# A two-branch transformer block on one core: early loads on one queue, eleven normalisations on GpSimd, a second value/key split, and a new order of work

## The chip, the cores and the metric

The kernel runs on one core of a Trainium2 chip. The core has a matrix engine (TensorE, "PE" in the profile, with its weight loads "PEld"), VectorE ("DVE"), ScalarE ("ACT"), GpSimd ("POOL"), SyncE ("SP", used here to issue DMAs), and 16 DMA engines. The metric is the device time of one execution in microseconds (us), lower is better. A difference of about 1% (2 us) is what a measurement of this kernel can tell from no change.

## What is computed

`x` is 2048 rows of 448 values (16 tiles of 128 rows, numbered 0 to 15 below). The block is a linear attention with softmax features, and then a gated MLP:

```
h  = x + attention(layernorm(x))
h2 = h + mlp(layernorm(h))

attention: q, k, v = split of x @ wqkv into 16 heads of 28
           phi(t)  = [softmax(t @ w_phi), softmax(-(t @ w_phi))]
           kv = sum over rows of phi(k)^T v ;  z = sum over rows of phi(k)
           o  = (phi(q) @ kv) / (phi(q) . z + 1e-6) ;  return o @ wo
mlp:       (sigmoid(x @ w_gate) * (x @ w_up)) @ w_down        inner width 1792
```

## The kernel before

The program is a graph of 887 named tasks. A task is written in this document by its name and numbers, as in `xn 7`. `_Graph.task` notes a task's engine (or, with `engs`, the engines that it may run on), what it depends on, and which PSUM banks it may take. `_Graph.stored` (line 132) reads the table `ORDER` (line 40): each number is 32 times the task's index, plus 4 times the number of the bank choice, plus the number of the engine choice. Dealt out by engine, the table gives the queue of each engine; an engine works its queue strictly in that order. `emit` (line 253) puts a semaphore wait before a task for each thing that it depends on. `TURNS` (line 90) adds pairs: the first task of a pair waits for the second as well, and nothing else depends on it. Within TensorE's queue waits are left out, except where the second half of a product follows its first half ("after", line 278).

The work goes through these stages.

The lead. Loads of `x` (`load_x`, in groups of two or four tiles), of the key, value and query columns of `wqkv` (`wk`, `wv`, `wq`), and of `w_phi` (`wph`) are issued on SP; three of them (`x 0`, `wk 1`, `x 6`) on ACT. The key and query weights are multiplied with `w_phi` once: TensorE transposes the key columns (`kT`, line 545), ACT copies them (`WkT`), TensorE multiplies (`wM`, line 560; `wM 1 b` for the keys, `wM 0 b` for the queries) with a masked `w_phi` (`Wp 0`, `Wp 1`, line 529), and ACT or VectorE copies the product out (`W2`). For a tile of `x`: statistics `bst`, `agg` on VectorE (588, 590), `ve` and `rstd` (591, 593: variance plus epsilon, to the power of -1/2, on GpSimd), the normalisation `xn` (line 608 on VectorE, 607 on ACT, which needs the negated mean `mm`, `nm` of lines 596 and 598), and the transpose into `xnT`: tiles 0 to 3 on TensorE (`xP`, 618) with a copy `xT`, the others in pairs by a DMA transpose on SP (`xT`, 626). TensorE's clock starts low, so dummy matmuls of a zero tile are put into its queue: `warm` (537) and 15 `fill` (993).

The key/value stage. `pair_of` (line 636) makes two products of 14 matmuls in all that run side by side on the two halves of the array, the first 8 as the task `pa` (or `va`) and the last 6 as `pb` (`vb`). A tile's key and value are one such pair; for the tiles in `VV` (line 584: tiles 0 and 1) the values of both tiles are one pair (`va 0`, `vb 0`) and the keys of both another (`pa 0`, `pb 0`). A pair takes two banks, which come free when what is in them has been read. Per tile follow `ekp`, `ekm` (exponentials, ACT), `v1` (a copy of the values), `ss` (sums, VectorE, 683), `rs` (687), `phi` (689, VectorE or GpSimd) and `kv` (16 matmuls into bank 4, line 701). Query products `qa`, `q` (741) for four tiles at a time and their exponentials `eqp`, `eqm` (751) run in between.

The bridge. After `kv 15`: `kvz` (756, VectorE), `num` (777: 16 matmuls for a tile), its copy `ocp` (line 784, ACT or VectorE), and for each pair of tiles `rSm`, `rr`, `b`, `c`, `rd`, `o` (lines 793 to 805, VectorE), the transpose of `o` (pair 0 on TensorE, `oP`, and `oT`; the others by DMA, `od` and `oT` on SP, 826), the product with `wo` (`woa`, `wo_`, 838), the residual and its statistics, `ve2`, `rstd2`, `hn`, and a second transpose (`hP`/`hT`, or `hT` on SP).

The MLP. `ga`, `gu` (939: gate and up, 70 pairs), `sig` (ACT), `hh` (956, VectorE), `dn` (973: 14 matmuls for a tile), `fin` (980, VectorE), `st` (the store, SP). The columns of the last tile's `dn 15` are cut in two (line 966), so that the first half is finished and stored while the second is computed.

Dealt out, the queues before begin as follows.

```
SP    x2 wk0 wph x4 wq2 wq3 wq1 wq0 x8 wv1 wv0 wom6 wqT1 wqT0 x12 wom4 xT4 ...
ACT   x0 wk1 x6 WkT3 WkT0 WkT1 WkT2 W2_1_3 W2_1_0 W2_1_2 W2_1_1 xT0 xT3 xT2 ekp0 ...
DVE   warm0 dmask bst3 bst2 agg3 agg2 ve2 bst1 bst0 Wp1 agg0 xn3 xn2 agg1 bst6 bst7 bst5
      xn0 xn1 agg6 bst4 xT1 agg5 agg4 agg7 ve4 mm4 bst8 ...
POOL  ... maskW rstd2 Wp0 ve0 ve1 rstd0 rstd1 rstd4 nm4 mm8 ve8 rstd8 kvz1 nm8 phi0 phi1 mm12
      rstd12 nm12 phi3 phi5 phi7 phi8 phi9 phi10 phi11
PE    warm0, 11 fills, kT3 kT0 kT1 kT2 wM13 wM10 wM11 xP3 wM12 fill xP0 xP1 kv0 xP2 3 fills
      pa0 pb0 pa3 va0 pb3 vb0 pa2 wM01 pb2 wM00 wM02 wM03 pa5 pa4 pb5 pb4 pa6 kv0 kv1 pb6 ...
```

Of the kernel before, what the change touches and what calls it, by code (L numbers as in the profile page):

```python
# [86 lines left out]
"""  # L87


TURNS = [(('phi', 0), ('xn', 8)), (('rstd', 12), ('xn', 11)), (('phi', 7), ('phi', 6)), (('phi', 11), ('phi',  # L90
         12)), (('rstd2', 2), ('hn', 2))]


class _Task:
    __slots__ = ("name", "eng", "occ", "lat", "fn", "deps", "rank", "kind", "banks", "until", "got",
                 "start", "finish", "idx", "bias", "need", "size", "after", "rows", "pace", "behind", "engs")


class _Graph:
# [934 lines left out]
```

## Time and profile before

| | |
|---|---|
| median of 3 runs | 205.72 us (205.47, 205.72, 206.79) |
| span of the profiled execution | 202.7 us (the profile gives no other time for it) |
| TensorE busy | 196.8 us, 97% of the span, 2279 matmuls |
| VectorE, ScalarE, GpSimd busy | 134.2, 93.3 and 31.2 us |
| chain of work that ended last | 91% TensorE, 4% VectorE, 2% DMA |
| first key/value product starts | 11.78 us |
| first gate product starts | 63.93 us |

The span is the time from the first to the last instruction of the profiled execution. The run's time is 3.0 us longer (205.72 less 202.7), for what lies around the span; the profiled execution is taken to be like the median one. Times in rows are us from the span's start. In a row of the timeline the two first columns are start and duration, then engine, line, operation, output and inputs, and how many instructions were merged; in brackets the idle time before, and what ended it.

### The profile page before, as it was taken

The numbers are of one execution on the slowest core, as the hardware profiler recorded it, in microseconds if no ns is written. First come the engines' busy times: TensorE is split into PE (matmuls) and PEld (weight loads), VectorE is DVE, ScalarE is ACT, GpSimd is POOL, SyncE is SP. The second block draws the span as 40 slices with busy tenths as digits, with TensorE's granted clock in tenths as the row PEclk, the third lists the DMA queues.
The fourth block names the chain that finished last, engine by engine and source line by source line (L and its number), as shares of the span: only waits on it lengthen the run. The fifth ranks groups of instructions, "written<-read, shape, count | busy, mean of one in ns | idle before, by whom it ended". The sixth has DMA issues, their size and how long they took to land.

```text
span 202.7 us, 5397 instructions
## 1 busy us (share of the span) xinstructions
PE 196.8 (97%) x2279; PEld 110.0 (54%) x2279; DVE 134.2 (66%) x305; ACT 93.3 (46%) x168; POOL 31.2 (15%) x51
## 2 busy tenths in 40 slices
PE   7899999998999999999999999999999999999994
PEld 2545554555347985555444444454444455895553
DVE  3999999987999985697968754443335305542132
ACT  2669998899999553343212432201352300442000
POOL 5526747720000110002000110000001000000000
PEclk9999999999999999999999999999999999999999
DMA  6998968733050097100262000040000500000222
GB/s 185 307 279 132 261 168 205 248 102 97 0 133 19 3 158 192 45 0 3 52 155 55 0 3 0 0 105 3 0 0 3 144 0 5 0 3 0 93 91 91
DMA packets 35109, 16.94 MB, mean 84 GB/s; under 512 B 26828, under 2 KB 34060, under 8 KB 35084
## 3 DMA queue, kind: packets, MB, share of 16 engines
q1 hardware_dynamic: 34460, 16.07, 32.5%
q10 hardware_dynamic: 624, 0.52, 0.8%
q8 instruction: 18, 0.29, 0.6%
q14 instruction: 7, 0.06, 0.1%
HBM read 8.98 MB, written 1.84 MB: 53 GB/s over the span
## 4 chain that ended last, share of the span: by engine, by line
PE 91%; DVE 4%; DMA 2%; issue 1%; SPq 0%
PE bank L939 42%; PE bank L973 21%; PE bank L642 11%; PE bank L838 5%; PE bank L741 5%; DMA wphd<-in_A_w_phi_dram 2%; PE bank L701 2%; PE bank L777 1%; DVE opm L430 1%; DVE st L588 1%; DVE xn_pad L608 1%; PE bank L560 0%; PE bank L618 0%; DVE rSm L793 0%; SPq L466 0%
## 5 line engine op out<-in xcount | busy, mean ns | idle before, releaser
L939 PE MATMUL bank<-xnT,wg_sb 64*128 64x512 bf16 (+1 forms) x490 | 87.6, 333 | 0.2 <-issue 0.2
L939 PE MATMUL bank<-xnT,wu_sb 64*128 64x512 bf16 (+1 forms) x490 | 87.6, 333 | 0.0
L948 ACT ACTIVATE sg_sb<-bank 128x512 f32<-128x512 f32 (+1 forms) x70 | 34.3, 514 | 80.8 <-PE bank L939 70.2
L956 DVE SCALAR_TENSOR_TENSOR hh<-sg_sb,bank 128x512 bf16<-128x512 f32 (+1 forms) x70 | 38.9, 575 | 29.2 <-ACT sg_sb L948 29.0
L939 PEld LDWEIGHTS bank<-xnT,wg_sb 64*128 64x128 bf16 x490 | 45.1, 94 | 18.9 <-issue 1.5
L939 PEld LDWEIGHTS bank<-xnT,wu_sb 64*128 64x128 bf16 x490 | 45.0, 94 | 15.4
L973 PE MATMUL bank<-wd_sb,hh 128*128 128x448 bf16 (+1 forms) x238 | 43.1, 342 | 0.0
L973 PEld LDWEIGHTS bank<-wd_sb,hh 128*128 128x128 bf16 x238 | 22.9, 98 | 20.1 <-issue 1.1
L980 DVE SCALAR_TENSOR_TENSOR x_sb<-bank,x_sb 128x448 bf16<-128x448 f32 (+1 forms) x17 | 9.9, 595 | 26.4 <-PE bank L973 26.4
L642 PE MATMUL bank<-Wk,xnT 64*128 64x448 bf16 x112 | 22.4, 350 | 0.1
L642 PE MATMUL bank<-Wv,xnT 64*128 64x448 bf16 x112 | 21.9, 350 | 0.0
L683 DVE TENSOR_REDUCE ssum<-ek 128x32 f32<-128x896 bf16 x16 | 16.6, 1060 | 0.5 <-ACT ek L662 0.4
L751 ACT ACTIVATE eq<-bank 128x1024 bf16<-128x1024 f32 x16 | 16.5, 1053 | 0.1
L689 POOL TENSOR_TENSOR phi<-ek,rsum 128x896 bf16<-128x896 bf16 x9 | 15.1, 1691 | 6.8 <-PE bank L701 2.9
L741 PE MATMUL bank<-xnT,Wq 64*128 64x512 bf16 x112 | 14.6, 377 | 0.6 <-ACT opm L430 0.5
L430 ACT CAST opm<-bank 128x960 bf16<-128x960 f32 x14 | 13.1, 979 | 1.0 <-PE bank L777 1.0
L878 POOL TENSOR_TENSOR rs<-rs,neghalf 128x2 f32<-128x2 f32 x8 | 5.5, 697 | 51.5 <-DVE rs L876 46.7
L838 PE MATMUL bank<-wo_sb,oT 64*128 64x448 bf16 x112 | 13.2, 350 | 0.0
L642 PEld LDWEIGHTS bank<-Wk,xnT 64*128 64x128 bf16 x112 | 9.1, 94 | 6.3 <-issue 0.6
L642 PEld LDWEIGHTS bank<-Wv,xnT 64*128 64x128 bf16 x112 | 9.2, 94 | 4.3
L588 DVE BATCH_NORM_STATS2 st<-x_sb 128x6 f32<-128x448 bf16 x16 | 9.1, 607 | 2.0 <-DMA x_sb<-in_A_x_dram 2.0
L664 ACT ACTIVATE ek<-bank 128x448 bf16<-128x448 f32 x16 | 9.2, 585 | 1.6 <-PE bank L642 1.6
(92 smaller groups left out, 168.6 us busy)
## 6 DMA issues: line engine op xcount, KB each, us to landing
...
wd_sb<-in_B_w_down_dram SPq DMA_DIRECT2D x7, 224.0 KB, 2.9
...
x_sb<-in_A_x_dram SPq DMA_DIRECT2D x2, 224.0 KB, 3.9
x_sb<-in_A_x_dram ACTq DMA_DIRECT2D x2, 224.0 KB, 4.0
```

The lines of the kernel that those rows point to most:

```text
L430: return e.copy(dst, src) if hasattr(e, "activation") else e.tensor_copy(dst, src)
L588: task(("bst", t), "dve", dve(D), lambda e, t=t: e.bn_stats(st1[:, t % 4, :], X(t)), [x_ld[t], opt(("agg", t - 4))])
L642: r = e.matmul(bank[bk][:, 0:D], lhsT=half(xnT, hi)[:, t, k, :], rhs=half(w, hi)[:, k, :], start=(i == 0), stop=(i == 6), tile_position=(6 ...
L683: task(("ss", t), "dve", dve(896), lambda e, s=s: e.tensor_reduce(ssum[:, s, :].rearrange("p (a h) -> p a h", h=2), ek[:, s].rearrange("p ...
L689: task(("phi", t), None, 1.68, lambda e, t=t, s=s: e.tensor_tensor(phi[:, t % NPHI, :, :, 0:DH, :].rearrange("p a g d h -> p (a g) d h"), ...
L741: r = e.matmul(bank[bb[j]], lhsT=half(Wq2, hi)[:, k, 2 * g:2 * g + 2].rearrange("p c d h -> p (c d h)"), rhs=half(xnT, hi)[:, 4 * c:4 * c ...
L751: task((key, gp, c), "act", act_p(1024), lambda e, gp=gp, c=c, sg=sg, nm=nm: e.activation(eq[c][:, sg, 2 * gp:2 * gp + 2, :], wide[got(nm) ...
L838: r = e.matmul(bank[bb[j]][:, 0:D], lhsT=half(oT, hi)[:, pr % NO, j, k, :], rhs=half(wo_sb, hi)[:, k, :], start=(i == 0 and not res), stop ...
L939: r = e.matmul(bank[b][:, 0:N], lhsT=half(w, hi)[:, k, fs], rhs=half(hnT, hi)[:, t0:t0 + n, k, :], start=(i == 0), stop=(i == 6), tile_pos ...
L948: task(("sig", f_, c), "act", act_p(N), lambda e, j=j, N=N, nm=nm: e.activation(sg_sb[:, j % NSG, 0:N], bank[got(nm)[0]][:, 0:N], ACT.Tanh ...
L956: task(("hh", f_, c), "dve", dve(N), lambda e, j=j, N=N, nm=nm, f_=f_, c=c: e.scalar_tensor_tensor(hhT[c % 2][:, f_, 0:N], sg_sb[:, j % NS ...
L973: r = e.matmul(bank[b][:, c0:c1], lhsT=hhT[c % 2][:, f_, o:o + P], rhs=wd_sb[:, f_, c0:c1], start=(f_ == 0), stop=(f_ == FT - 1))
```

## The change

- All early loads are issued on SP: `x 0`, `wk 1` and `x 6` leave ACT. Their order is new, and `wv` comes before half of `wq`.
- `xn` of tiles 4 and up may run on GpSimd, as multiply and add with `rs1` and `nm1`. The table puts eleven there (tiles 5 to 15); nine of them were on VectorE and two on ACT. `xn 4` goes from VectorE to ACT. Tiles 10 to 15 now wait for the transpose that last read their buffer.
- `VV` becomes (0, 2): tiles 2 and 3 too have a pair of values and a pair of keys.
- 22 dummies instead of 15: after `warm`, 14 stand before the first product (5 ahead of the small product `kv0`, 4 behind it, 5 between `kT`, `wM` and `xP`), 4 between `vb 2` and `pb 2`, 3 behind `kv 15`, 1 behind `oP`.
- `b`, `c` and `o` may run on GpSimd; the table puts `c 0`, `b 3`, `c 3`, `o 3`, `b 4`, `c 4` there.
- Nine of the `phi` are on VectorE (7 before), seven on GpSimd (9 before).
- The cut of the last tile is at column 336 instead of 224.
- `ORDER` and `TURNS` are new. From `h 3` on (about 75 us) the queues of PE and DVE are the old ones, with other banks. The loads `wd` go behind `oT 4` on SP.

```diff
-NFILL = 15
+NFILL = 22
...
+TURNS = [(('Wp', 0), ('xn', 1)), (('xn', 12), ('phi', 1)), (('phi', 9), ('phi', 8)), (('phi', 13), ('phi', 12)),
+         (('c', 0), ('b', 0)), (('b', 3), ('hn', 1)), (('b', 4), ('hn', 5))]
...
-        load(("wk", 1), wk_raw[0:64, 3, :], A_wqkv[3 * P:D, D:2 * D], bias=BIG, size=56.0, engs=("act", "sp"))
+        load(("wk", 1), wk_raw[0:64, 3, :], A_wqkv[3 * P:D, D:2 * D], bias=BIG, size=56.0)
...
-        VV = (0,)
+        VV = (0, 2)
...
+                    if K.tasks[("xn", t)].eng == "pool":
+                        return e.tensor_scalar(dst, src, rs1[:, t:t + 1], nm1[:, t:t + 1], op0=ALU.mult, op1=ALU.add)
...
-                     engs=("dve",) if a < 4 else ("act", "dve"))
+                     engs=("dve",) if a < 4 else ("act", "dve", "pool"))
...
+        for t in range(NXP, NT):
+            last = ("xT", t - NXP if t - NXP in PE_X else (t - NXP) // 2 * 2)
+            K.tasks[("xn", t)].deps.append(last)
+            K.tasks[("xn", t)].need.append(last)
...
-                deps.append(("pb", min(4 * c + 3, NT - 1)))
+                deps.append(k_at[min(4 * c + 3, NT - 1)][2])
...
-            task(("c", pr), "dve", dve(464), lambda e, both=both, s2=s2: e.tensor_tensor(
+            task(("c", pr), None, dve(464), lambda e, both=both, s2=s2: e.tensor_tensor(
...
-                    cuts = [(0, D)] if tt < NT - 1 else [(0, D // 2), (D // 2, D)]
+                    cuts = [(0, D)] if tt < NT - 1 else [(0, 336), (336, D)]
```

Dealt out, the new table's queues begin as follows (`f` is a dummy).

```
SP    x0 x2 wk0 wph wk1 x6 x4 wq1 wv1 wq0 wv0 x8 wq2 wq3 x12 wqT0 wqT1 xT4 wom6 xT6 xT8 wg0 xT10 ...
ACT   WkT0 WkT1 WkT3 WkT2 W2_1_0 xT0 W2_1_3 W2_1_1 xT2 xn4 v1_1 v1_0 ekp1 ekm1 ekp0 ekm0 v1_3 W2_0_2 v1_2
      W2_0_3 W2_0_1 W2_0_0 ekm3 ekm2 ekp2 ekp3 ekp5 ...
DVE   warm0 bst1 bst0 agg1 bst3 bst2 agg0 agg2 agg3 Wp1 dmask xn1 bst7 bst6 bst5 agg7 xn0 agg6 agg5 bst4
      xn3 agg4 xn2 xT1 W2_1_2 xT3 bst9 bst8 bst10 agg10 bst11 ... bst15 ... ss0 ss1 rs0 rs1 phi0 phi1 ss3
      rs3 ss4 ss5 rs4 rs5 ss2 v1_7 rs2 ss6 ss7 rs6 rs7 phi7 ss9 phi5 phi6 ...
POOL  ... z_phi epsT ident ve1 rstd1 v1one ve0 rstd0 ve2 kvz1 Wp0 rstd2 ve4 mm4 rstd4 nm4 xn7 xn5 xn6 ve8
      rstd8 nm8 xn8 xn9 xn11 xn10 mm12 ve12 rstd12 nm12 xn12 xn13 phi3 xn15 phi4 phi2 xn14 phi9 phi10
      phi11 phi13 c0 ve2_0 rstd2_0 b3 c3 o3 rstd2_1 rstd2_2 b4 c4 ...
PE    warm0 5f kv0 4f kT0 kT1 f kT3 f kT2 wM10 f xP1 xP0 wM13 wM11 wM12 f xP3 f xP2 va0 pa0 vb0 pb0 va2
      pa2 vb2 2f wM02 2f wM00 wM03 wM01 pb2 pa5 pa4 pb5 pb4 pa6 kv_0 kv_1 pb6 pa7 qa00 pb7 q00 pa9 pa8 pb9
      pb8 pa10 kv_2 kv_3 kv_4 pb10 ... kv_15 3f num1 num0 num5 qa03 num2 num3 num4 q03 qa02 qa12 num7 q12
      q02 oP1 oP0 f wr0 woa0 num6 wo_0 qa13 q13 woa1 wo_1 num9 woa2 ...
```

More of the change, by code (lines that the diff above doesn't have):

```diff
@@ L40 @@
 ORDER = """
[46 rows of a table removed]
-"""
-TURNS = [(('phi', 0), ('xn', 8)), (('rstd', 12), ('xn', 11)), (('phi', 7), ('phi', 6)), (('phi', 11), ('phi',
-         12)), (('rstd2', 2), ('hn', 2))]
[47 rows of a table added]
+"""
+TURNS = [(('Wp', 0), ('xn', 1)), (('xn', 12), ('phi', 1)), (('phi', 9), ('phi', 8)), (('phi', 13), ('phi', 12)),
+         (('c', 0), ('b', 0)), (('b', 3), ('hn', 1)), (('b', 4), ('hn', 5))]
 class _Task:
@@ L489, in build @@
         load(("wk", 0), wk_raw[:, 0:3, :], A_wqkv[0:3 * P, D:2 * D].rearrange("(a p) n -> p a n", p=P), bias=BIG,
-             size=336.0, engs=("act", "sp"))
-        load(("wk", 1), wk_raw[0:64, 3, :], A_wqkv[3 * P:D, D:2 * D], bias=BIG, size=56.0, engs=("act", "sp"))
+             size=336.0)
+        load(("wk", 1), wk_raw[0:64, 3, :], A_wqkv[3 * P:D, D:2 * D], bias=BIG, size=56.0)
         load("wph", wphd[:], A_w_phi.rearrange("h i j -> (h i) j").rearrange("(a p) j -> p a j", p=GP), bias=BIG - 1,
@@ L494, in build @@
         for h_ in range(2):
-            load(("wv", h_), Wv[:, 2 * h_:2 * h_ + 2, :], rows_of(A_wqkv, 2 * D, D, h_), bias=BIG - 4 - h_, size=224.0,
-                 engs=("act", "sp"))
-        load_x(2, 4, bias=BIG - 3, engs=EITHER)
-        load_x(4, 6, bias=BIG - 7, engs=EITHER)
-        load_x(6, 8, bias=BIG - 8, engs=EITHER)
+            load(("wv", h_), Wv[:, 2 * h_:2 * h_ + 2, :], rows_of(A_wqkv, 2 * D, D, h_), bias=BIG - 4 - h_, size=224.0)
+        load_x(2, 4, bias=BIG - 3)
+        load_x(4, 6, bias=BIG - 7)
+        load_x(6, 8, bias=BIG - 8)
         load_x(8, 12, bias=BIG - 9)
@@ L601, in build @@
                 s = t % NXP
-                free = opt(("xT", t - NXP if t - NXP in PE_X else (t - NXP) // 2 * 2))
                 def f(e, t=t, s=s):
@@ L607, in f @@
                         return e.activation(dst, src, ACT.Identity, bias=nm1[:, t:t + 1], scale=rs1[:, t:t + 1])
+                    if K.tasks[("xn", t)].eng == "pool":
+                        return e.tensor_scalar(dst, src, rs1[:, t:t + 1], nm1[:, t:t + 1], op0=ALU.mult, op1=ALU.add)
                     return e.tensor_scalar(dst, src, mv1[:, t, 0:1], rs1[:, t:t + 1], op0=ALU.subtract, op1=ALU.mult)
-                task(("xn", t), None, dve(160), f, [("rstd", a), opt(("nm", a)), free],
-                     engs=("dve",) if a < 4 else ("act", "dve"))
+                task(("xn", t), None, dve(160), f, [("rstd", a), opt(("nm", a))],
+                     engs=("dve",) if a < 4 else ("act", "dve", "pool"))
         xT_of = {}
@@ L796, in build @@
                 rr[:, s2], rSm[:, s2], both(0)[:, :, :, E - 1, :], ALU.mult), [("rSm", pr), opt(("b", pr - 2))])
-            task(("b", pr), "dve", dve(464), lambda e, both=both, s2=s2, fac=fac: e.tensor_tensor(
+            task(("b", pr), None, dve(464), lambda e, both=both, s2=s2, fac=fac: e.tensor_tensor(
                 b_sb[:, s2], both(1)[:, :, :, 0:EV, :], fac(rr[:, s2], EV), ALU.mult),
-                [("rr", pr), opt(("o", pr - 2))])
-            task(("c", pr), "dve", dve(464), lambda e, both=both, s2=s2: e.tensor_tensor(
+                [("rr", pr), opt(("o", pr - 2))], engs=("dve", "pool"))
+            task(("c", pr), None, dve(464), lambda e, both=both, s2=s2: e.tensor_tensor(
                 b_sb[:, s2].rearrange("p t g e j -> p t g (e j)"), b_sb[:, s2].rearrange("p t g e j -> p t g (e j)"),
-                both(0)[:, :, :, 0:EV, :].rearrange("p t g e j -> p t g (e j)"), ALU.add), [("b", pr)])
+                both(0)[:, :, :, 0:EV, :].rearrange("p t g e j -> p t g (e j)"), ALU.add), [("b", pr)], engs=("dve", "pool"))
             task(("rd", pr), "dve", dve(256), lambda e, s2=s2: e.reciprocal(
                 rden[:, s2], b_sb[:, s2, :, :, EV - 1, :]), [("c", pr), opt(("o", pr - 2))])
-            task(("o", pr), "dve", dve(448), lambda e, pr=pr, s2=s2, fac=fac: e.tensor_tensor(
+            task(("o", pr), None, dve(448), lambda e, pr=pr, s2=s2, fac=fac: e.tensor_tensor(
                 o_pad[:, pr % NO, :, 0:D].rearrange("p t (g d j) -> p t g d j", g=G, j=HL), b_sb[:, s2, :, :, 0:DH, :],
-                fac(rden[:, s2], DH), ALU.mult), [("rd", pr), opt(("oT", pr - NO)), opt(("oT", pr - NO, 0)), opt(("oT", pr - NO, 1))])
+                fac(rden[:, s2], DH), ALU.mult), [("rd", pr), opt(("oT", pr - NO)), opt(("oT", pr - NO, 0)), opt(("oT", pr - NO, 1))], engs=("dve", "pool"))
             if pr in PE_O:
```

93 rows, old and new, of the table ORDER are left out of this document.

## The prediction

> **What bounds the kernel now.** I read the page first, then the chain of work that ended last, then the timelines of the lead, of the bridge and of the tail. The page:
>
> ```profile
> span 202.7 us, 5397 instructions
> PE 196.8 (97%) x2279; PEld 110.0 (54%) x2279; DVE 134.2 (66%) x305; ACT 93.3 (46%) x168; POOL 31.2 (15%) x51
> ...
> DVE  3999999987999985697968754443335305542132
> ...
> GB/s 185 307 279 132 261 168 205 248 102 97 0 133 19 3 158 192 45 0 3 52 155 55 0 3 0 0 105 3 0 0 3 144 0 5 0 3 0 93 91 91
> ```
>
> TensorE is busy for 97%, and it computes the same products after the change. VectorE is full in the first third. The chain in order of time:
>
> ```profile
> 1.79 4.95 DMA wphd<-in_A_w_phi_dram
> ...
> 11.20 0.65 PE bank L993 x3
> ...
> 17.90 0.70 PE bank L560 x12
> ...
> 18.64 3.60 PE bank L642 x36
> ...
> 27.18 1.32 PE bank L642 x14
> ...
> 63.93 5.96 PE bank L939 x106
> ...
> 74.05 0.76 PE bank L838 x8
> ...
> 183.79 16.05 PE bank L973 x98
> ...
> 199.86 0.39 DVE x_sb L980
> ```
>
> From the first product at 11.8 to 199.8 nearly every piece is TensorE (those left out are of this kind too, but for some 8 us between 47 and 64), 188 us in all. So time can be won or lost at three places only: before the first product, in stalls up to the MLP, and behind the last product. A key/value pair costs 1.32, a warm dummy 0.65/3 = 0.22, a `wM` task of four matmuls 0.2 (12 in 0.70, with the end of the last).
>
> **The change, part by part.** The median of the runs is 205.72, the span 202.7: 3.0 lies around it, and I keep that. I sum changes of the span.
>
> *1. The lead.* Its rows:
>
> ```profile
> 0.79 0.45 SPq L466 DMA_DIRECT2D x_sb<-in_A_x_dram  x1
> 0.79 0.48 ACTq L466 DMA_DIRECT2D x_sb<-in_A_x_dram  x1
> ...
> 1.31 0.53 ACTq L466 DMA_DIRECT2D wk_raw<-in_A_wqkv_dram  x1
> 1.44 4.89 PE L993 MATMUL bank<-warm 128*128 128x512 bf16 x11
> ...
> 1.56 0.27 DVE L455 TENSOR_REDUCE dmask<-ident 128x2 f32<-128x112 bf16 x1 [0.57 <-POOL neghalf L439]
> 1.79 0.49 SPq L466 DMA_DIRECT2D wphd<-in_A_w_phi_dram  x1
> ...
> 3.78 1.15 DVE L588 BATCH_NORM_STATS2 st<-x_sb 128x6 f32<-128x448 bf16 x2 [1.96 <-DMA x_sb<-in_A_x_dram]
> ...
> 6.76 0.39 DVE L529 TENSOR_TENSOR Wp<-wphd,maskW 112x224 bf16<-112x224 bf16 x1 [0.35 <-DMA wphd<-in_A_w_phi_dram]
> ...
> 10.86 0.40 DVE L430 COPY xnT<-bank 128x512 bf16<-128x512 bf16 x1
> ...
> 11.18 0.30 DVE L590 BATCH_NORM_AGGREGATE mv<-st 128x2 f32<-128x6 f32 x3
> ...
> 11.78 1.74 PE L642 MATMUL bank<-Wk,xnT 64*128 64x448 bf16 x14
> ...
> 12.78 0.30 PEld L642 LDWEIGHTS bank<-Wk,xnT 64*128 64x128 bf16 x6 [0.50 <-PE bank L642]
> ```
>
> The first product waits for VectorE's chain from the landing of `x` (3.78) to `xT 1` (10.86 to 11.26), and then for the three dummies of the chain's row at 11.20. (a) Two loads of `x` share the DMA engines at 0.79; now `x 0` goes alone and `x 2` follows 0.5 later. Statistics begin at about 3.3: -0.5 (between 0 and -0.7, the whole of a 224 KB load at the 307 GB/s of the page's second slice). (b) The wait of 0.35 for `wph` goes: by then VectorE has eight more instructions queued (to about 5.9), and `wph` is no longer crossed by a load on ACT's queue: -0.35 (0, if it lands as late as now). (c) Ahead of `xT 1` VectorE gets `dmask` (0.2 of its 0.27 once overlapped) and three `agg` (0.1 each, 0.30 for three) and loses `ve 2` (0.1): +0.4. So `xT 1` ends at 10.8 instead of 11.26. (d) Between it and the first product stands `xP 2` alone, not three dummies: `va 0` at about 10.95 instead of 11.78. The lead gives -0.83. Issuing costs SP half a microsecond each, so `wk 1`, third after `wk 0`, goes out near 2.8 instead of 1.31; `kT` needs it only at about 5.95, behind the nine cold dummies (0.43 each, the row of 11 at 1.44) and `kv0`. ACT loses three issues of about 0.5, where it had no other work yet: 0.
>
> *2. The products up to `pa 5`.* Before, from 11.78 to 18.64 (the chain's row of 36), 6.86. Now four pairs at 1.32, four `wM` 0.79, four dummies 0.86, two changes of shape 0.2: 7.15, +0.29. `pb 0` right behind `pa 0` cost a stall: 8 of the 14 matmuls of 1.32, 0.75, stood until 12.78, 1.00 later; nothing is adjacent so now, and the 7.15 has none of it. The dummies cover a wait: `wM 0 2` takes bank 6 when ACT has read `pa 0` (about 16.0, four exponentials after `pb 0`). Removing them would therefore not return 0.86. A later fusion of `kv 5` with 6 to 8 saves two changes of shape: -0.2.
>
> *3. Normalisations on GpSimd.* No row shows `xn` there. The nearest:
>
> ```profile
> 1.50 0.49 POOL L461 MEMSET zsel<- 128x464 bf16 x1
> ...
> 6.80 0.77 POOL L529 TENSOR_TENSOR Wp<-wphd,maskW 112x224 bf16<-112x224 bf16 x1 [0.64 <-DMA wphd<-in_A_w_phi_dram]
> ...
> 11.76 1.01 POOL L593 TENSOR_TENSOR rs<-rs,neghalf 128x4 f32<-128x4 f32 x1 [2.19 <-DVE nm L596]
> ...
> 18.63 3.34 POOL L689 TENSOR_TENSOR phi<-ek,rsum 128x896 bf16<-128x896 bf16 x2 [1.10 <-DVE xn_pad L608]
> ```
>
> ```profile
> 13.99 1.27 SPq L626 DMA_TRANSPOSE xnT<-xn_pad  x1
> ```
>
> The clear gives 0.84 ns an element beyond 0.1, `phi` (1.69 for 896) 1.8 with two inputs, `Wp` 3.0 with runs of two. For 512 elements: 0.53, 1.0, 1.6. `xn` has one tensor input in runs of 256: nearest to the clear, I take 0.7. GpSimd's queue then reads: `nm 4` 11.85 (`agg 4` on VectorE near 9.95, then `ve`, `mm` and `nm` at 0.2 and `rstd` at 1.01); `xn 7, 5, 6` to 13.95; `ve 8`, `rstd 8` (1.01), `nm 8` 15.15+; four `xn`; the same three for tiles 12 to 15, to 20.05; `xn 12` waits for `phi 1` (20.4); `xn 13` 21.8, `phi 3` 23.5, `xn 15`, `phi 4` 25.9, `phi 2` 28.1. TensorE asks for `phi 2` (`kv 2`, now behind `pa 10`) at about 28.95: `pa 5` at 18.1 and 10.9 of products. So the cost is 0, with 0.85 of cover. With c for one `xn`, `phi 2` ends at 20.2 + 10c; above c = 0.88 every 0.1 costs 1 us. Transposes: `xT 4` goes out at 13.2, 0.8 earlier than in the row at 13.99, and `xT 6` after it; `xT 14` at about 28.9, landing by 32.5, wanted at 35.8. VectorE loses nine `xn` and gains two `phi`; TensorE does not wait for it in this stage. `kv 15` comes at -0.83 + 0.29 - 0.2, about 0.75 earlier.
>
> *4. GpSimd beside VectorE.*
>
> ```profile
> 40.34 1.69 POOL L689 TENSOR_TENSOR phi<-ek,rsum 128x896 bf16<-128x896 bf16 x1 [0.61 <-DVE phi L689]
> ```
>
> ```profile
> 41.78 0.74 DVE L689 TENSOR_TENSOR phi<-ek,rsum 128x896 bf16<-128x896 bf16 x1
> ...
> 43.89 0.62 DVE L689 TENSOR_TENSOR phi<-ek,rsum 128x896 bf16<-128x896 bf16 x1
> ```
>
> A `phi` on VectorE that began 0.25 before one on GpSimd ended took 0.74 instead of 0.62. [...] I take 0, from the rows; the upper bound is one `rstd`, 1.0.
>
> *5. The bridge.*
>
> ```profile
> 46.14 0.64 DVE L756 TENSOR_TENSOR kvz<-bank,dmask 128x464 bf16<-128x464 f32 x1 [0.71 <-PE bank L701]
> ...
> 51.34 0.58 DVE L800 TENSOR_TENSOR b_sb<-b_sb,opm 128x928 bf16<-128x928 bf16 x1
> ...
> 53.39 0.34 PE L813 MATMUL bank<-ident,o_pad 128*128 128x128 bf16 x3 [0.30 <-DVE o_pad L805]
> ```
>
> Three dummies stand where `qa03` was, in the wait for `kvz`: 0. The query products move ahead of `oP`, into its waits. But `oP` follows a chain of VectorE, `ocp 0`, `rr 0`, `b 0`, `c 0`, `rd 0`, `o 0`, and `woa 1` the DMA transpose of `o 1`; neither gets shorter. `c 0` goes to GpSimd at 1.75 (928 elements by the rate of `phi`) instead of 0.58; VectorE does `ocp 3` (1.15), two `rSm` and two `rr` meanwhile, as much, so `rd 0` comes at the same place. `woa 1` and its second half become adjacent (+0.25, as `pa 0` and `pb 0`), q12 is gone from ahead of `woa 0` (up to -0.35): together -0.1. `b 3`, `c 3`, `o 3` at 1.75 each run from about 61.5 to 68 beside `h` and the first `hh`, and `b 4`, `c 4` from 71 to 75; `woa 3`, which wants the first three, stands at 74.05 (chain). Queued behind them on GpSimd are `rstd2 1` and `rstd2 2`, for the gate products of tiles 2 to 5 near 76. `wd` moves behind `oT 4` on SP, seven issues near 77, wanted by the first `dn`, after 28 gate pairs. All 0; without that cover a GpSimd instruction here costs its 1.75.
>
> *6. The tail.*
>
> ```profile
> L980 DVE SCALAR_TENSOR_TENSOR x_sb<-bank,x_sb 128x448 bf16<-128x448 f32 x15 | 9.2, 622 | 25.3 <-PE bank L973 25.3
> ...
> L980 DVE SCALAR_TENSOR_TENSOR x_sb<-bank,x_sb 128x224 bf16<-128x224 f32 x2 | 0.8, 392 | 1.1 <-PE bank L973 1.1
> ```
>
> ```profile
> 198.52 0.92 DVE L980 SCALAR_TENSOR_TENSOR x_sb<-bank,x_sb 128x224 bf16<-128x224 f32 x2 [0.72 <-PE bank L973]
> 199.86 0.39 DVE L980 SCALAR_TENSOR_TENSOR x_sb<-bank,x_sb 128x224 bf16<-128x224 f32 x1 [0.42 <-PE bank L973]
> ```
>
> (The row at 198.52 merges `fin 15` with `fin 12`, which is queued behind it.) With the cut at 336, `fin 15` can start 0.65 later (112 columns, 14 times 47 ns), at 199.2, and takes 0.51; `fin 12` (0.62, overlapping by 0.1) ends at 200.2, and the last `fin` (112 columns, about 0.28) at 200.4 instead of 200.25. SP must issue `st 12` (0.45, as its rows above) ahead of the last store, which so goes out near 200.65; before, it could as soon as the row at 199.86 had ended, at 200.25. +0.35 (between -0.1, for the shorter last piece, and +0.5).
>
> Sum: -0.83 + 0.29 - 0.2 - 0.1 + 0.35 = -0.5, so a span of 202.2 and a time of 205.2.
>
> **The rivals.**
>
> *GpSimd becomes the bound.* For: its queue has no gap from 10 to 28 us, and `Wp` ran at 3.0 ns an element. Against: `xn` has long runs. At c = 1.2, between `phi`'s rate and that of `Wp`, `phi 2` ends at 32.2 and TensorE waits 3.3 us: 208.5. It is slower by over 1% from c = 1.13.
>
> *The loads land later.* One queue issues what two did. `wph` goes out at 2.3 instead of 1.79; if it takes its 4.95 again, it lands at 7.25, and `Wp 1`, now ahead of the first `xn`, holds VectorE for 1.4: 206.6, no change that can be told. Against: its delay had a load on the other queue in it.
>
> *More is won.* If the sharing cost the full 0.7, the bridge gives 0.35, and the tail nothing: -0.2 - 0.25 - 0.35 less, 204.4; and if the dummies of step 2 cover more than the wait for bank 6, down to 203.5.
>
> [...]
>
> **How the numbers follow.** Forecast (204.5 to 206.0): 0.54. GpSimd-bound (from 207.0): 0.15. Late loads (206.0 to 207.2): 0.13. More won (203.2 to 204.5): 0.18. The range 203.8 to 207.4 leaves out most of the first rival and a third of the last, about 0.19. Faster by over 1% is below 203.66, 0.10 from the last rival; slower is above 207.78, 0.14; within 1%, which is what a measurement of this kernel can tell from no change, 0.76.
>
> **What would show it.** `bst 1` at 3.3; no wait at `Wp`; the first product (`va 0`) at 10.95 and `pa 5` near 18.1; `xn` on GpSimd at 0.7; `kv 2` without a wait; the first gate product near 63.1 instead of 63.93; the last `fin` ending 0.15 later against the last matmul than now, and the span 0.35. The forecast is wrong if `xn` takes over 0.9 on GpSimd, if `wph` holds VectorE, or if TensorE shows a new wait between 18 and 45.

## The result, and the profile after

The changed kernel takes 206.42 us (median of 11 runs, 205.85 to 207.75), the kernel before on the same chip 205.36 (11 runs, 204.35 to 206.79). The ratio is 1.0081, 95% interval 1.0061 to 1.0102: 0.8% slower, where 0.2% faster was forecast. A ratio here compares undisturbed executions alone, so it need not equal the quotient of the medians, which take in all.

From the page of the changed kernel (the lines that answer to those of before, and the clock that was granted, in tenths):

```profile
span 204.0 us, 5416 instructions
PE 197.8 (97%) x2286; PEld 109.3 (54%) x2286; DVE 131.5 (64%) x290; ACT 92.3 (45%) x164; POOL 48.7 (24%) x70
...
PEclk9799999999999999999999999999999999999999
...
PE 95%; DMA 2%; issue 1%; DVE 1%; SPq 0%; DVEq 0%
```

The second slice of the clock is a 7; before it was 9 throughout. The DMA in the chain, 2% as before, is now the load of `wk` and no longer that of `wph`. TensorE's timeline of the lead (idle time ahead of a row, and its releaser, in brackets):

```profile
3.96 1.25 PE L998 MATMUL bank<-warm 128*128 128x512 bf16 x4
6.73 0.98 PE L545 MATMUL bank<-ident,wk_raw 128*112 128x128 bf16 x8 [1.52 <-DMA wk_raw<-in_A_wqkv_dram]
7.64 0.48 PE L998 MATMUL bank<-warm 128*128 128x512 bf16 x1
7.91 0.75 PE L545 MATMUL bank<-ident,wk_raw 128*112 128x128 bf16 x4
8.60 0.61 PE L998 MATMUL bank<-warm 128*128 128x512 bf16 x1
...
12.84 0.36 PE L647 MATMUL bank<-Wv,xnT 64*128 64x448 bf16 x2
```

The four dummies behind `kv0`, all but the first at full clock, were done at 5.2; `wk 0` landed at 6.17 (5.30 before) and `wk 1` at 6.63 (5.50 before), and `kT` needs both; TensorE stood for 1.52. Now the same stretch by windows (the column behind the five engines is the granted clock), and below it the window behind the rise of the clock in the kernel before:

```profile
4.39:7.80 3.41, 1.89 (x13) 1.06 (x12) 3.11 (x11) 0.53 (x2) 2.51 (x7) 1.00 1.03 268
7.80:11.22 3.42, 3.42 (x23) 2.44 (x22) 3.03 (x12) 2.02 (x5) 1.88 (x6) 0.50 1.12 328
```

```profile
6.18:9.59 3.41, 3.22 (x38) 2.44 (x36) 3.06 (x9) 2.90 (x7) 2.23 (x5) 1.00 1.15 291
```

In the changed kernel the clock rose at 4.39, and at 7.80 it was taken back to half for 3.4 us; before, it rose at 6.18 and stayed. In those 3.4 us the `kT`, `wM`, `xP` and the dummies between them are the chain (its first row is `wk 0`):

```profile
1.79 4.38 DMA wk_raw<-in_A_wqkv_dram
...
6.73 0.98 PE bank L545 x8
7.70 0.41 PE bank L998
8.11 0.55 PE bank L545 x4
...
10.66 0.77 PE bank L619 x8
11.44 0.59 PE bank L560 x12
```

VectorE, which ended the lead before, now waits for TensorE ahead of `xT 1`:

```profile
6.42 0.39 DVE L529 TENSOR_TENSOR Wp<-wphd,maskW 112x224 bf16<-112x224 bf16 x1 [0.30 <-DMA wphd<-in_A_w_phi_dram]
...
11.13 0.42 DVE L431 COPY xnT<-bank 128x512 bf16<-128x512 bf16 x1 [0.39 <-PE bank L619]
```

The first product comes at 12.84 instead of 11.78, +1.06. Starts in the two traces give the rest: `pa 5` 20.02 (18.64 before), `kv 15` 46.81 (45.68), the first gate product 65.02 (63.93). The end, VectorE's last pieces, before and then after:

```profile
197.18 0.62 DVE L980 SCALAR_TENSOR_TENSOR x_sb<-bank,x_sb 128x448 bf16<-128x448 f32 x1 [1.49 <-PE bank L973]
```

```profile
198.13 0.62 DVE L985 SCALAR_TENSOR_TENSOR x_sb<-bank,x_sb 128x448 bf16<-128x448 f32 x1 [1.49 <-PE bank L978]
200.13 1.22 DVE L985 SCALAR_TENSOR_TENSOR x_sb<-bank,x_sb 128x336 bf16<-128x336 f32 x3 [1.37 <-PE bank L978]
```

From the first of these rows to the end of the span it is 5.5 before (202.7) and 5.9 after (204.0).

### The profile page after: what moved, and what is told of

The parts are those of the page before. It is cut to its first block, busy times and chain, and to the rows that moved or that the text cites. A ratio compares the mean times of both kernels' runs of the same rounds, so it can differ in the third digit from the quotient of the medians.

```text
span 204.0 us, 5416 instructions
## 1 busy us (share of the span) xinstructions
PE 197.8 (97%) x2286; PEld 109.3 (54%) x2286; DVE 131.5 (64%) x290; ACT 92.3 (45%) x164; POOL 48.7 (24%) x70
## 4 chain that ended last, share of the span: by engine, by line
PE 95%; DMA 2%; issue 1%; DVE 1%; SPq 0%; DVEq 0%
PE bank L944 42%; PE bank L978 21%; PE bank L647 11%; PE bank L746 6%; PE bank L843 5%; PE bank L706 2%; DMA wk_raw<-in_A_wqkv_dram 2%; PE bank L782 2%; PE bank L998 2%; PE bank L545 1%; PE bank L560 1%; PE bank L619 1%; DVE x_sb L985 1%; SPq L467 0%; PE bank L897 0%
## 5 line engine op out<-in xcount | busy, mean ns | idle before, releaser
L978 PE MATMUL bank<-wd_sb,hh 128*128 128x448 bf16 (+2 forms) x238 | 43.1, 342 | 0.0
L978 PEld LDWEIGHTS bank<-wd_sb,hh 128*128 128x128 bf16 x238 | 22.4, 98 | 20.7 <-issue 1.1
L985 DVE SCALAR_TENSOR_TENSOR x_sb<-bank,x_sb 128x448 bf16<-128x448 f32 (+2 forms) x17 | 9.8, 594 | 26.7 <-PE bank L978 26.7
L647 PE MATMUL bank<-Wv,xnT 64*128 64x448 bf16 x112 | 20.7, 350 | 0.0
L647 PE MATMUL bank<-Wk,xnT 64*128 64x448 bf16 x112 | 20.5, 349 | 0.0
L881 POOL TENSOR_SCALAR rs<-mv 128x2 f32<-128x2 f32 x3 | 0.6, 192 | 62.9 <-DVE mv L879 55.2
L746 PE MATMUL bank<-xnT,Wq 64*128 64x512 bf16 x112 | 14.1, 376 | 0.1
L694 POOL TENSOR_TENSOR phi<-ek,rsum 128x896 bf16<-128x896 bf16 x7 | 11.7, 1689 | 7.9 <-ACT ek L669 4.9
```

The lines of the kernel that those rows point to most:

```text
L647: r = e.matmul(bank[bk][:, 0:D], lhsT=half(xnT, hi)[:, t, k, :], rhs=half(w, hi)[:, k, :], start=(i == 0), stop=(i == 6), tile_position=(6 ...
L694: task(("phi", t), None, 1.68, lambda e, t=t, s=s: e.tensor_tensor(phi[:, t % NPHI, :, :, 0:DH, :].rearrange("p a g d h -> p (a g) d h"), ...
L746: r = e.matmul(bank[bb[j]], lhsT=half(Wq2, hi)[:, k, 2 * g:2 * g + 2].rearrange("p c d h -> p (c d h)"), rhs=half(xnT, hi)[:, 4 * c:4 * c ...
L978: r = e.matmul(bank[b][:, c0:c1], lhsT=hhT[c % 2][:, f_, o:o + P], rhs=wd_sb[:, f_, c0:c1], start=(f_ == 0), stop=(f_ == FT - 1))
L985: task(("fin",) + nm[1:], "dve", dve(c1 - c0), lambda e, nm=nm, tt=tt, pr=pr, c0=c0, c1=c1: e.scalar_tensor_tensor(X(tt)[:, c0:c1], bank[g ...
```

## Experiments

The theory: with one queue `wk` lands late, TensorE lets a stretch pass with too little work, its clock is taken back, and its cold lead becomes the chain; the tail adds its 0.4. Rival A: the late `wk` alone is the loss. Rival B: the dummies between the lead's products cost their own time. The table has all runs. "Down" counts executions whose mean granted clock was under 0.997; "first" is the start of the first product in the profiled one (blank where it is not given).

| kernel | median us | ratio to before (95%) | down | first |
|---|---|---|---|---|
| changed kernel | 206.42 | 1.0081 (1.0061 to 1.0102) | 9 of 11 | 12.84 |
| e1 two queues | 205.37 | 1.0033 (1.0008 to 1.0059) | 3 of 12 | 11.45 |
| e2 seven more dummies | 205.39 | 1.0048 (1.0025 to 1.0070) | 0 of 10 | 12.07 |
| e3 before, one queue | 205.31 | 1.0029 (1.0014 to 1.0044) | 2 of 7 | 11.80 |
| e4 cut 224 | 206.50 | 1.0042 (1.0002 to 1.0083) | 6 of 12 | 14.40 |
| e5 no lead dummies | 206.96 | 1.0088 (1.0062 to 1.0114) | 11 of 12 | 13.10 |
| e6 two queues, dummies in waits | 205.81 | 1.0025 (0.9991 to 1.0058) | 3 of 12 | 11.30 |
| e7 = e6, no product dummies | 205.60 | 1.0026 (1.0000 to 1.0052) | 0 of 12 | 11.65 |
| e8 one queue, dummies ahead | 205.30 | 1.0030 (1.0003 to 1.0058) | 0 of 12 | 11.14 |
| e9 = e8, wq early | 207.60 | 1.0103 (1.0049 to 1.0157) | 1 of 6 | 11.23 |
| e10 = e9, no product dummies | 207.28 | 1.0105 (1.0066 to 1.0145) | 2 of 6 | 11.31 |
| e11 before, cut 336 | 205.16 | 1.0032 (1.0004 to 1.0059) | 2 of 12 | 11.63 |
| e12 = e8, wq ahead of x 8 | 206.21 | 1.0031 (1.0002 to 1.0060) | 0 of 12 | 11.43 |
| e13 two queues, wq ahead of x 8 | 206.34 | 1.0044 (1.0013 to 1.0075) | 1 of 13 | |
| e14 = e13, no product dummies | 205.39 | 1.0021 (0.9992 to 1.0050) | 1 of 12 | 11.28 |
| e15 = e14, o 4 ahead of h 3 | 206.55 | 1.0055 (1.0024 to 1.0086) | 2 of 12 | 12.34 |
| e16 = e14, bridge of before | 205.23 | 1.0008 (0.9978 to 1.0037) | 4 of 12 | |
| e17 before, h 3 ahead of o 4 | 205.99 | 1.0061 (1.0035 to 1.0087) | 1 of 12 | 11.96 |
| e18 one queue, bridge of before | 204.91 | 0.9995 (0.9967 to 1.0022) | 0 of 12 | 11.27 |

### The lead: e1, e2, e3, e5

e1, queues (`-` changed kernel, `+` experiment):

```diff
-SP  x0 x2 wk0 wph wk1 x6 x4 ...
+SP  x2 wk0 wph x4 ...
+ACT x0 wk1 x6 ...
```

> The changed kernel with its early loads back on two queues as before: x 0, wk 1 and x 6 on ACT, then x 2, wk 0, wph, x 4 on SP; all else as changed. Theory (TensorE runs dry while it waits for wk, and its clock is taken back): wk lands at about 5.5 instead of 6.63, kT 0 starts near 5.9 or right behind the dummies, the idle stretch before it falls from 1.52 to under 0.8, no 3.4 us at half the clock follow, and the first product comes at about 11.4 instead of 12.84, held by VectorE's xT 1 again. Time about 205.0, ratio to the kernel before 0.998 (0.995 to 1.002) instead of 1.008. Rival A (only the later kT counts, not the clock): 0.8 us less, 205.6, ratio 1.004, and the stretch at half the clock stays or plays no part. Rival B (the dummies between the lead's tasks or their order cost the time): kT earlier helps little, ratio 1.006 to 1.008.

e2, TensorE's queue:

```diff
-... kv0 4 dummies kT0 ...
+... kv0 11 dummies kT0 ...
```

> The changed kernel with seven more dummies right ahead of kT 0; the loads stay on one queue, so wk lands as late as in the changed kernel. Theory (clock): the dummies fill the stretch 5.2 to 6.7, the clock stays up once it is up, kT starts at about 6.7 as before, but the tasks behind it run at 0.22 to 0.47 instead of 0.43 to 0.7: the first product at about 11.4, time about 205.0 to 205.4, ratio 0.998 to 1.001. Where the clock rises late, the seven dummies take 3.0 instead of 1.5 and kT starts up to 1 us later; the median should still gain. Rival A (late loads): kT is as late as in the changed kernel or later, ratio 1.008. Rival B (dummies cost TensorE's time): ratio 1.008 to 1.012.

e3, the kernel before:

```diff
-SP  x2 wk0 wph x4 ...
-ACT x0 wk1 x6 ...
+SP  x0 x2 wk0 wph wk1 x6 x4 ...
```

> The kernel before with its seven early loads on SP alone, in the order of the changed kernel (x 0, x 2, wk 0, wph, wk 1, x 6, x 4); everything else as before. Theory (clock): wk lands at about 6.6, the twelve dummies last to 6.3, so TensorE stands only 0.3 to 0.5 before kT, the clock is not taken back, and VectorE's chain still ends the lead: statistics at 3.57 instead of 3.78, and no wait for wph beyond what is left of it; ratio 0.997 to 1.002. Rival A (the late wk itself is the loss): kT, WkT and wM come 0.6 later and so does the first product: ratio 1.003 to 1.004.

e5, TensorE's queue:

```diff
-kT0 kT1 f kT3 f kT2 wM10 f xP1 xP0 wM13 wM11 wM12 f xP3 f xP2
+kT0 kT1 kT3 kT2 wM10 xP1 xP0 wM13 wM11 wM12 xP3 xP2
```

> The changed kernel without its five dummies between kT, wM and xP (loads on one queue, kT 0 still behind a wait of 1.5 us). Theory (clock): the clock is taken back as in the changed kernel, or more often, since still less runs through TensorE behind the wait; what is gained is only the room of the dummies, five at 0.22 to 0.43 or 1.1 to 2.1 us in TensorE's queue, of which about 1 us can count before VectorE's xT 1 ends the lead again. First product 11.4 to 12.2, time 205.4 to 206.2, ratio 1.003 to 1.007, and the mean granted clock under 0.995 in a third of the runs or more. Rival B (the dummies themselves cost the time, the clock nothing): ratio 0.998 to 1.001 and little scatter.

e2 leaves the loads as late as they were and adds work to TensorE, and still gains: `kT 0` started at 7.43, 0.7 later than in the changed kernel, and the first product at 12.07, 0.8 earlier. That is against rivals A and B, though its ratio, 1.0048, missed the theory's 0.998 to 1.001. In e5 five dummies less gained nothing: the clock was down in 11 of 12 executions, in the profiled one to 0.983 in the mean (the theory had 1.003 to 1.007 and a first product by 12.2). That is against B again. The times of e1 and e3 don't decide: 1.0033 and 1.0029 are what rival A forecast (1.004; 1.003 to 1.004), and the theory's 0.998 and 0.997 to 1.002 were missed. Their traces do speak against A: in e1's the clock stayed up and the first product came at 11.45 (theory 11.4), and in e3 `wk 1` landed at 6.80 and the lead stood all the same (first product at 11.80, 11.78 before). What e3 lost came later: `pa 5` waited 0.38 (the profile names a copy of ACT, but `xT 4`, which it needs too, landed at 18.95 instead of 17.79, 0.05 ahead of it); no theory had named that.

What takes the clock back? Not busy time by the profile alone. Stretches of 3.41 us, as long as the one at half clock in the changed kernel, of e5, e4 and e3:

```profile
3.81:7.22 3.41, 1.27 (x8) 0.49 (x6) 2.81 (x11) 0.00 (x0) 2.08 (x6) 1.00 1.00 257
```

```profile
3.96:7.37 3.41, 1.67 (x12) 0.85 (x10) 3.07 (x12) 0.09 (x1) 2.25 (x5) 1.00 1.00 268
7.37:10.78 3.41, 3.41 (x20) 2.15 (x19) 3.31 (x11) 2.25 (x5) 1.84 (x6) 0.50 1.11 329
10.78:14.20 3.42, 3.42 (x30) 2.87 (x29) 1.48 (x4) 1.73 (x4) 3.21 (x6) 0.50 1.24 254
```

```profile
3.80:7.21 3.41, 1.66 (x10) 0.66 (x8) 3.04 (x8) 0.00 (x0) 1.27 (x2) 1.00 1.03 270
```

Behind e3's 1.66 the clock stayed (1.00 from 7.21 to 10.62), behind the changed kernel's 1.89 it fell to 0.50; and in e4 a stretch at 0.50 with TensorE busy throughout (7.37 to 10.78) was followed by another at 0.50. Nor does the wait for `wk` alone tell: e3's TensorE stood 1.7 for it, the changed kernel's 1.52. My estimate is that busy time hides how little a `kT` streams: before, the sixteen matmuls of the four `kT` took 1.93 (from 6.13) for 1792 columns, where a warm dummy takes 0.22 for 512. No run tried that by itself; what takes the clock back was not shown.

When the clock rises differs between the profiles (at 4.39 in the changed kernel's, at 6.18 in that of the kernel before), and the same lead wins or loses: e4, whose lead is the changed kernel's, had a median of 204.5 us in its six executions with the clock up (204.2 to 206.1) and 207.0 in four of the six with it down (206.9 to 207.2). The changed kernel's own executions don't show it so clearly: its two with the clock up took 205.92 and 206.39, its nine with it down 205.85 to 207.75. The kernel before is not safe from it either: in the executions measured beside the experiments its clock was down in 10 of 155, and these took 206.75 to 207.89.

### The tail: e4, e11

```diff
-cuts = [(0, D)] if tt < NT - 1 else [(0, 336), (336, D)]
+cuts = [(0, D)] if tt < NT - 1 else [(0, 224), (224, D)]
```

> The changed kernel with the last tile cut at column 224 again instead of 336; all else as changed. The step for the tail as it was predicted: 0.35 less than the changed kernel (0.38 by the two traces), time 206.05, ratio to the kernel before 1.0063 instead of 1.0081. Rival (the last store and not the cut sets the end): no difference, ratio 1.008.

e11 is the kernel before with 336 in place of 224.

> The kernel before with the last tile cut at column 336 instead of 224; all else as before. The step for the tail as it was predicted: 0.35 slower (0.38 by the two traces), ratio 1.0018. Rival (shorter last piece, the store not in the way): 0.1 faster, ratio 0.9995.

The clock's scatter covers the effect in e4's ratio; in the traces it is plain. Of e4:

```profile
199.72 0.63 DVE L985 SCALAR_TENSOR_TENSOR x_sb<-bank,x_sb 128x448 bf16<-128x448 f32 x1 [1.49 <-PE bank L978]
```

To its span's end (205.3) it is 5.6, as in the kernel before (5.5); in e11 it is 5.9 (197.20 to 203.1), as in the changed kernel. So the cut costs 0.4, and e11's ratio, 1.0032, holds the 1.0018 that was expected in its interval.

### Clock and tail mended: e6, e8; the dummies among the products: e7

e6 has e1's queues, e8 the changed kernel's; both are cut at 224.

```diff
-kv0 4f kT0 kT1 f kT3 f kT2 wM10 f xP1 xP0 wM13 wM11 wM12 f xP3 f xP2
+kv0 5f kT0 kT1 kT3 kT2 4f wM10 xP1 xP0 wM13 wM11 wM12 xP3 xP2   (e6)
+kv0 9f kT0 kT1 kT3 kT2 wM10 xP1 xP0 wM13 wM11 wM12 xP3 xP2      (e8)
```

> The changed kernel with its early loads on two queues, the five dummies taken from between the lead's products and put into its two waits (one ahead of kT 0, four ahead of the first wM), and the tail's cut at 224. Theory (clock): TensorE never passes too little in one window of 3.4 us, so the clock stays up in every run once it is up, and a cold start is caught up in the waits; the first product at about 11.3 in all runs (VectorE's xT 1 ends the lead). Time about 204.1 (the two-queue kernel's lowest runs, 204.6, less 0.1 for the first product and 0.38 for the tail), ratio 0.997 (0.995 to 0.999), scatter under 1 us. Rival A (only late loads counted): the same as the two-queue kernel less the tail, ratio 1.001 with its scatter of 204.2 to 206.5.

> The changed kernel with its early loads on one queue, as changed, but the five dummies moved from between the lead's products to right ahead of kT 0, and the tail's cut at 224. Theory (clock): the wait for wk is covered, the clock stays up, and VectorE, whose statistics start at 3.57 instead of 4.09 in the two-queue kernel, ends the lead: first product at about 11.0, time about 203.9, ratio 0.996 (0.994 to 0.999), mean clock 0.997 or more in all runs. Rival A (the late wk is the loss): the first product stays at 12 or later, ratio 1.003 or more. Rival B (the dummies cost their own time): ratio 1.004 as for the changed kernel with this cut.

```diff
-vb2 2f wM02 2f wM00 wM03 wM01 pb2
+vb2 wM02 wM00 wM03 wM01 pb2
```

> As the kernel with two queues and its dummies in the waits, but without the four dummies (0.86 us) among the first key and value products. The step as it was predicted: they cover a wait of wM 0 2 for bank 6, which ACT frees, so removing them returns 0 to 0.3 of the 0.86. Rival: they are simply time on TensorE's queue and the whole 0.86 comes back: ratio lower by 0.004.

TensorE's lead in e8:

```profile
3.96 3.47 PE L998 MATMUL bank<-warm 128*128 128x512 bf16 x9
7.26 1.90 PE L545 MATMUL bank<-ident,wk_raw 128*112 128x128 bf16 x16
...
11.14 0.93 PE L647 MATMUL bank<-Wv,xnT 64*128 64x448 bf16 x8
```

e8 shows the clock's part most cleanly: `wk 1` as late as in the changed kernel (6.55), the same number of dummies, no wait ahead of `kT`, and the first product at 11.14. The clock was up in all 36 executions of e8, e12 and e18, which have this lead, and down in 26 of the 35 of the changed kernel, e4 and e5. (e9 and e10 have it too and lost the clock in 3 of 12; there TensorE waited 2.3 and 2.8 later on, which may be why.) In e6, with two queues, the clock was still down in 3 of 12, against the forecast. And neither became as fast as forecast (0.997 for e6, 0.996 for e8); e8's 1.0030 is not clear of e4's 1.0042. e7 shows one reason: 0.86 us of dummies less, and nothing came back. TensorE's waits in e7 between 11 and 20:

```profile
PE bank L560 <- DMA WqT<-wq_raw: 0.8, 1, 0.8
PE bank L560 <- ACT Wq L431: 0.2, 1, 0.2
```

The dummies cover a DMA, the transposes of `WqT`, which landed at 13.6 before and at 17.8 in the changed kernel; not bank 6.

### WqT earlier: e9, e10, e12, e13, e14

```diff
-SP ... wq1 wv1 wq0 wv0 x8 wq2 wq3 x12 wqT0 wqT1
+SP ... wv1 wv0 wq2 wq3 wq1 wq0 x8 wqT1 x12 wqT0   (e9; e10 as e7's diff)
+SP ... wv1 wv0 wq2 wq3 wq1 wq0 x8 x12 wqT1 wqT0   (e12; e13 on two queues)
```

> As the kernel with one queue and its dummies ahead of kT 0 (ratio 1.003), but on SP the four loads of wq and the first of the two DMA transposes of WqT come ahead of x 12, wv ahead of wq. Theory (a third loss behind the clock and the tail): the change moved the transposes of WqT from landing at 13.6 to 16 to 17.8, wM 0 waits for them, and with it all that follows; with wq early they land by about 15.5, wM 0 2 starts at about 16.5 without a wait for a DMA, and the time falls by 0.4 to 0.9: 204.2 to 204.7, ratio 0.998 to 1.001. Rival (WqT is covered, and wM 0 waits for bank 6 as it was predicted): no difference, ratio 1.003; a second rival is x 12, now later, which could hold VectorE's statistics of tiles 12 to 15: slower by up to 1.

> As the kernel with wq early, without the four dummies (0.86 us) among the first key and value products. Theory: the dummies only covered the wait for WqT; with WqT landed by 15.5 most of the 0.86 comes back, about 0.5 to 0.8: ratio 0.995 to 0.998. Rival, the step as it was predicted (bank 6, which ACT frees at about 16.0): 0 to 0.3 comes back.

> As the kernel with one queue, its dummies ahead of kT 0 and the cut at 224 (ratio 1.003; WqT landed at 16.95 and wM 0 2 waited 0.36 for it). On SP, wv and the four loads of wq now come ahead of x 8 and x 12, and the two DMA transposes of WqT behind x 12, so that no plain load waits behind a transpose. Theory (WqT is the third loss): both transposes land by about 16, wM 0 2 starts at about 16.4 without a wait for a DMA, and the time is 0.4 to 0.6 lower: 204.3, ratio 0.999 (0.997 to 1.002), clock up in all runs. Rival (the wait was a matter of that one execution, or x 8, now later, holds VectorE): ratio 1.003 or more.

e13 has 4 more dummies ahead of `kT 0` and 3 ahead of `wM10`; e14 drops the four among the products.

> The same order of wv, wq, x 8, x 12 and WqT, with the early loads on two queues, four dummies put ahead of kT 0 and three ahead of the first wM, cut at 224. Theory: more columns stream in each window than in the two-queue kernel before it, of whose twelve runs three showed a mean clock of 0.992; so the clock stays at 0.997 or more in all runs, WqT lands by about 15.5 and is not waited for; first product at 11.3 to 11.5; time about 204.2, ratio 0.998 (0.996 to 1.001). Rival (the scatter has another source): runs above 206 stay, ratio 1.0025.

> As the kernel before it in this call, without the four dummies (0.86 us) among the first key and value products. Theory (the dummies cover the wait for WqT): with WqT landing at 15.5 about 0.5 to 0.8 comes back, ratio lower by 0.0025 to 0.004. Rival, the step as it was predicted (they cover a wait for bank 6, which ACT frees at about 16.0): 0 to 0.3 comes back, and wM 0 2 waits for ACT. Second rival: WqT still lands later than the four dummies would end, and wM 0 2 waits for the DMA: nothing comes back.

Four of the five missed their numbers clearly; e14's ratio is 0.0023 below e13's (forecast 0.0025 to 0.004), which is within the noise. That more columns stream in e13 is an estimate; its clock was down in 1 of 13, against the forecast. In e9 `wqT 0`, now behind `x 12`, landed at 19.04 and not at 16.95 as in e8, and `wM 0` started at 19.09: the wait grew from 0.4 to 2.3, and the time with it (1.0103).

```profile
PE bank L560 <- DMA WqT<-wq_raw: 2.3, 1, 2.3
```

e12 still waited 0.8 and e14 0.4, so none of the orders tried for it brought both transposes ahead of 16.6. Whether the four dummies would come back with `WqT` early stays open.

### The bridge: e15, e16, e17, e18

With the clock up, e8 still scattered from 204.4 to 207.0. The profiled execution of e12 shows a wait that the changed kernel's own did not have:

```profile
80.23 1.23 SPq L831 DMA_TRANSPOSE oT<-o_pad  x1
```

```profile
85.14 0.93 PE L843 MATMUL bank<-wo_sb,oT 64*128 64x448 bf16 x8 [1.28 <-DMA oT<-o_pad]
```

That is `oT 4`, which `woa 4` wants. Before, it was issued at 77.11, landed at 80.0 and was wanted at 82.67, 2.6 to spare:

```profile
77.11 1.23 SPq L826 DMA_TRANSPOSE oT<-o_pad  x1
```

```profile
82.67 0.75 PE L838 MATMUL bank<-wo_sb,oT 64*128 64x448 bf16 x6
```

In the changed kernel `b 4` and `c 4` stand on GpSimd until 76.3, `rd 4` and `o 4` behind `h 3` on VectorE, and the transpose goes out late:

```profile
80.46 1.32 SPq L831 DMA_TRANSPOSE oT<-o_pad  x1
```

It landed at 83.2 and was wanted at 83.72: 0.5 to spare. From issue to landing it took 2.7 to 3.7 in seventeen of the twenty profiles, and 4.9, 4.5 and 4.8 in those of e12, e13 and e14.

```diff
-DVE ... h3 rd4 o4 rSm5 rr5 od4   (e14)
+DVE ... rd4 o4 h3 rSm5 rr5 od4   (e15)
```

> As the two-queue kernel with wq early and without the product dummies (ratio 1.0021), with one change of VectorE's order: rd 4 and o 4 go ahead of h 3 instead of behind it. In the changed kernel o 4 ends at 79.8 (76.6 before), its DMA transpose is issued at 80.5 and lands 2.6 later, 0.5 ahead of woa 4; in three of the executions it took 4.7 and woa 4 waited 0.9 to 1.3. Theory (this thin cover is a fourth loss, in part of the executions): the transpose goes out near 76.5, woa 4 never waits, and the runs above 205.8 become rare; median 204.8, ratio 0.999 to 1.001. Rival (the scatter has another source, or h 3, now later, is wanted at once): ratio 1.002 or more.

e17 moves `h 3` the other way in the kernel before (ahead of `rd4 o4 hh120`). e16 has, from the end of `kv 15` on, every queue as before; e18 the same behind e8's lead, without product dummies and with `pb 2` ahead of `wM 0`.

> The kernel before with one change: on VectorE h 3 goes ahead of rd 4 and o 4, as in the changed kernel, so that the transpose of o 4 goes out about 2 us later (80 to 80.5 instead of 77.1), while woa 4 still stands at 82.7. Theory (thin cover): where the transpose takes 2.6 nothing changes, where it takes 4.7 woa 4 waits 1 to 2; lowest runs as before, median 0 to 0.8 higher, ratio 1.001 to 1.004. Rival (the cover never mattered): ratio 1.000.

> As the same kernel, but from the end of the key and value stage on with the orders of the kernel before on all engines: b 3, c 3, o 3, b 4, c 4 and c 0 on VectorE again, no dummies in the wait for kvz, q12 and the query products in their old places, wd loaded early, tail cut at 224. What is left of the change is its lead (mended) and its products with eleven xn on GpSimd. Theory: the new bridge costs a wait in part of the executions and wins nothing else, so this is as good as the kernel with o 4 ahead of h 3 or better: ratio 0.998 to 1.000 (kv 15 came 0.27 earlier than before in the profile of the parent). Rival (the bridge as changed is worth its 0.26 at woa 0): 1.000 to 1.002.

> What the runs so far leave standing of the change, put together: the early loads on one queue as changed, the five dummies ahead of kT 0 (in that lead the clock stayed up in twelve of twelve runs), no dummies among the first products, the second half of the keys of tiles 2 and 3 ahead of wM 0 instead of four dummies, eleven xn on GpSimd as changed, then the bridge and the tail of the kernel before. Theory: clock up in all runs; no wait for WqT over 0.4; kv 15 at 44.9 to 45.5 (45.68 before), no wait of woa 4; time 0.2 to 0.7 below the kernel before, ratio 0.997 to 0.999, and little scatter. Rival A (the products stand against the loads and xT 4, whatever goes ahead): kv 15 at 45.7, ratio 1.000 to 1.002. Rival B (the scatter belongs to the lead or to xn on GpSimd and not to the bridge): runs above 206 stay, ratio 1.002 to 1.004.

e15 failed as an experiment: the transpose also waits for `od 4`, which `h 3` now held up, and went out at 80.1 all the same. e17 is confounded: `h 3` held up `hh 12 0`, and TensorE waited 1.2 for that bank, not for `oT 4`. e16 pointed the right way, with its two-queue clock mixed in: its eight executions with the clock up took 204.4 to 205.8. In e18, with the old bridge, eleven of twelve executions lie between 204.73 and 205.32, where e8 had five of twelve at 206 or above, and the ratio is 0.9995. Its `oT 4` went out at 77.56. Taken over the runs, and with the clock up alone: with the old bridge (e16, e18) 1 of 20 executions took 206 or more, with the new bridge and the same leads (e8, e12, e14) 14 of 35, and the kernel before 6 of 145. So the new bridge costs some 0.3%, by executions in which it waits. That size is rough, since the intervals of e8 and e18 overlap and e18 also lost the four dummies among the products (which in e7 gained nothing) and got another place for `pb 2`; that `oT 4` is the whole of it is likely, not shown. e18's products were not won: `kv 15` came at 46.13 (forecast 44.9 to 45.5, 45.68 before). e18 stands with the kernel before; no version beat it.

## Why the prediction was wrong

*Step 1 failed, and in it "`kT` needs it only at about 5.95".* It counted the dummies at 0.43, cold. Where the clock rises early, they run at 0.22 and end at 5.2; and `wk` landed not before 5.95 but at 6.63. The step gave `wk 1` an issue (2.8) but no landing: with the 4.2 that it took before (1.31 to 5.50) it lands at 7.0, behind even the cold dummies, so the wait could have been read from the trace of the kernel before. (a) was less than half as large (statistics at 3.57 instead of 3.78, forecast 3.3); (b) did not come (`wph` landed at 6.40, the wait at `Wp 1` is still 0.30); and with TensorE at half clock, (c) and (d) no longer ended the lead. -0.83 became +1.06.

*The clock* has no term in the sum. Behind the stretch without `wk` it was 0.50 for 3.4 us, and with the late `wk` the lead came 1.06 later than before in the profile; e4's executions with the clock down (0.983 to 0.992 in the mean) took 2.5 more than those with it up. In the sum VectorE stayed the chain.

*Step 2* was right in size, +0.32 to `pa 5` (forecast +0.29) and -0.25 from there to `kv 15` (-0.2), and wrong in what the dummies cover (bank 6 for `WqT`); the size came out because TensorE's own times fill the stretch either way. *Step 3* was right; the group of the eleven `xn` (busy time and mean ns behind the bar):

```profile
L608 POOL TENSOR_SCALAR xn_pad<-x_sb,rs,nm 128x512 bf16<-128x512 bf16 x11 | 8.3, 768 | 0.3
```

One took 0.77 (forecast 0.7), `phi 2` ended at 30.41 and `kv 2` stood at 31.11 without a wait, both over 2 later than forecast, most of it the late lead. (The queue as the step lists it gives 27.6 for `phi 2` and not 28.1, as 25.9 and one `phi` of 1.69; the cost is 0 by both.) *Step 4*: a `phi` on VectorE beside an `xn` on GpSimd took 1.00 instead of 0.62 where the two overlapped for 0.53 (from 30.63), behind cover: 0, as taken; the upper bound of one `rstd`, 1.0, is shown by no run. *Step 5* was near for the profiled execution (-0.04, forecast -0.1) and, by e8, e12, e16 and e18, wrong over many: "without that cover a GpSimd instruction here costs its 1.75" was the clause to follow to `oT 4`, whose cover fell to 0.5. *Step 6*: +0.37, forecast +0.35.

The terms of the profile, 1.06 + 0.32 - 0.25 - 0.04 + 0.37, less 0.13 in the MLP, give the 1.3 of the spans. One slip beside it: the 3.0 around the span took the profiled execution for a median one; the later profiles have 1.8 (e1: 204.53 for a span of 202.7), so that the same spans would have given a forecast 1.2 lower and further off.
